# Key and value products cut into two parts, statistics cut from their combination, and new orders for all five engines, in a one-core transformer block

## The chip, the core and the metric

The kernel runs on one core of a Trainium2 chip. Its time is the device time of one execution in microseconds; the median of three runs is the number compared. The core has five engines that run side by side and meet at semaphores: PE (TensorE, matrix products, with its weight loads shown apart as PEld), DVE (VectorE), ACT (ScalarE), POOL (GpSimd) and SP (SyncE, which here only issues DMAs). PE writes to PSUM, eight banks of 512 numbers per partition, from which DVE and ACT read.

## What is computed

The input is a matrix x of 2048 rows (tokens) and 640 columns in bfloat16. A block of linear attention is followed by a dense block, each with a layer norm before it and the input added after it:

```python
h  = x + A(layernorm(x))          # A: linear attention, 32 heads of 20
h2 = h + B(layernorm(h))          # B: silu(h @ w1) @ w2, 1728 wide

def A(x):
    q, k, v = split(x @ wqkv)                     # each 2048 x 640
    pq, pk  = q @ w_phi, k @ w_phi                # per head, 20 x 20
    phi_q   = concat(softmax(pq), softmax(-pq))   # 40 numbers per head
    phi_k   = concat(softmax(pk), softmax(-pk))
    kv, z   = phi_k.T @ v, sum over rows of phi_k # per head 40 x 20 and 40
    return ((phi_q @ kv) / (phi_q @ z)) @ wo
```

## The kernel before

**Tiles.** The tokens are 16 tiles of 128. A tile number is the first number of most steps. The 640 columns are five pieces of 128 where they are contracted over.

**One long list of steps.** The whole program is the string ORDER (L25 to L68): some 620 words, each a call of a small function op_xx, with its arguments behind dots and the PSUM banks it takes behind "@". The words are run from left to right, and each instruction goes to the end of its own engine's queue. Every engine works its queue strictly in that order, so ORDER holds five orders at once, written out in full; only the order of words of the same engine counts. A word whose operand isn't ready holds up all later words of its engine.

**The weights.** wk, wv, wo, w1 and w2 are loaded in pieces (lk, lv, lo, l1, l2; the last rows of w2 by lh) and x in groups of tiles (lx); a last "s" or "a" names the issuing queue, SP or ACT. The small matrices w_phi are folded into the key weights: wt.c transposes piece c of wk on PE (L320), wc.c copies it out of PSUM (L326), ph builds a block-diagonal form of w_phi on DVE (L197) with a mask from mk on POOL, fk.c multiplies the two on PE (L329), and fc.c copies the product to Wfk on ACT (L350). For the queries lq.c loads the weights transposed by DMA, into the same memory as wk (wTq is wk, L135), so lq has to wait until every wt has read wk; gk and gc then do what fk and fc do.

**The layer norm of x.** st.t takes the statistics of the two halves of a tile and combines them, on DVE (L270). rs.a.b makes the reciprocal root of the variance of tiles a to b-1: an add (on DVE for one tile, on POOL for two), then a power and products on POOL (L276 to L291). xn.t normalises, on DVE ("v") or ACT ("a") (L293). Then the tile is transposed: xd.t by a DMA of SP (L313), or xt.t on PE (L304) and xc.t out of PSUM (L310).

**Keys and values.** kp.t and vp.t are the projections of a tile (proj, L366): five pieces times two halves of 320 columns, ten matmuls into a pair of banks. Each of them reads its piece of the transposed tile and of Wfk or wv. ke.t takes the exponentials of both signs on ACT (L392), kr.t their sums per head and the reciprocals on DVE (L401), kn.t the product with them; a letter says how it is shared between POOL and DVE: "p" all on POOL, "q", "b" and "d" three quarters, half and one quarter on POOL, "v" all on DVE (L409). vc.t copies the values out of PSUM. cc.t adds the tile's product of keys and values into bank 7, which collects them over all tiles (L422). kc and km bring the sum into the form used later, with a mask from mt.

**Queries, attention, dense block.** qp, qs, qr and qt are the query projections of four tiles each (L462 to L473), qe their exponentials. dp.t is the product of queries with keys and values, into four banks; dw, dr and do form the quotient (DVE, DVE, DVE or POOL), td transposes it by DMA, op.t multiplies it with wo on PE, and oa.t adds x (DVE). sq, sr, hn and hd are the second layer norm and its transpose. up.g.k are the products with w1 for a group of tiles, ua the silu on ACT, yp and yh the products with w2, yo and yz the last addition and the store.

**Fillers.** wm.n is a product of ones with n columns into an unused bank (L266); eight of 512 columns and six of 256 stand among the first steps.

Of the kernel before, what the change touches and what calls it, by code (L numbers as in the profile page):

```python
# [35 lines left out]
xd.12 vp.12@6 vc.12.v kr.3 kn.3.p kp.4@0 xn.15.a ke.4 kp.12@4 cc.9 cc.1 kr.4 kn.4.p cc.0 xn.14.v cc.11 ke.5
kr.5 kn.2.d xd.13 ke.12 kr.12 lq.4.s xd.6 kp.6@0 lq.0.s ke.6 vp.13@2 vc.13.a kp.13@4 ke.13 vp.6@0 xd.15
xd.10 gk.4@2 vp.10@4 vc.6.a lq.3.s gk.3@0 gc.4.a gc.3.a vc.10.a kn.5.q kp.10@2 kn.12.p kr.6 xn.7.a l1.3.s
kn.6.q lq.1.s gk.1@0 gc.1.a kr.13 kn.13.p cc.4 cc.5 l1.0.s ke.10 kr.10 cc.2 cc.3 cc.12 xd.14 xd.7 kr.8
kn.8.p kn.10.d vp.15@4 vc.15.a kp.15@0 ke.15 kp.14@2 gk.0@4 gc.0.a vp.7@0 ke.14 kr.14 kn.14.p qp.0.1@4  # L40
qs.0.1 qr.0.1 kp.7@2 ke.7 l2.10.13.s kr.15 l1.2.s cc.8 vc.7.v cc.13 l2.2.4.s cc.10 qt.0.1 qp.0.0@2 qs.0.0
kn.15.p qr.0.0 qt.0.0 qe.0.1 l2.4.6.s kr.7 kn.7.v l2.6.8.s qe.0.0 vp.14@0 vc.14.a qp.0.2@6 qs.0.2 cc.6 cc.7
mt qe.0.2 cc.15 cc.14 kc km.0 lh.s qp.3.0@4 qs.3.0 qr.3.0 km.1 dp.0@0 l1.4.s close dw.0.p dr.0 qt.3.0
do.0.1.p qe.3.0 qp.2.0@6 qs.2.0 qr.2.0 qt.2.0 qe.2.0 do.0.0.p dp.1@0 dw.1.p qp.1.0@4 dr.1 do.1.0.p qs.1.0
qr.1.0 qt.1.0 qe.1.0 qp.1.1@6 td.0 do.1.1.p td.1 dp.3@0 dw.3.p dr.3 do.3.0.p qs.1.1 qr.1.1 qt.1.1 qe.1.1
qp.3.2@4 qp.1.2@5 dp.2@0 dw.2.p qs.1.2 qe.1.2 do.3.1.p td.3 qs.3.2 op.0@6 dr.2 do.2.1.p do.2.0.p qe.3.2 oa.0
dp.4@0 dw.4.p td.2 sq.0 qp.2.2@5 qs.2.2 qe.2.2 op.1@6 oa.1 sr.0 qp.2.1@4 dp.6@0 dw.6.p l1.5.s l1.1.s qs.2.1
qr.2.1 hn.0.a hd.0 sq.1 qt.2.1 sr.1 hn.1.v hd.1 qe.2.1 op.3@6 oa.3 sq.3 dp.5@0 dw.5.p op.2@4 sr.3 oa.2
hn.3.a sq.2 dr.5 do.5.0.p do.5.1.p qp.3.1@6 qs.3.1 l2.0.2.s l2.8.10.s qr.3.1 dp.9@0 dw.9.p td.5 dr.9
do.9.0.p dr.6 do.6.1.p dr.4 do.4.1.p do.4.0.p td.4 qt.3.1 qe.3.1 up.0.2@4 ua.0.2 dp.7@0 sr.2 up.0.0@6 ua.0.0  # L50
dw.7.p dr.7 up.0.3@4 ua.0.3 do.6.0.p dp.8@0 dw.8.p dr.8 hn.2.a up.0.1@6 ua.0.1 td.6 do.8.0.p op.5@4 oa.5
dp.12@0 dw.12.p dr.12 yp.1.0@6 do.7.1.p do.7.0.p sq.5 td.7 hd.3 op.4@4 oa.4 sr.5 hn.5.v hd.5 do.9.1.p sq.4
td.9 sr.4 hn.4.a dp.10@0 dw.10.p yp.1.1 yp.0.1@4 yh.0.0 hd.2 hd.4 yo.1 dp.11@0 dw.11.p dr.11 do.8.1.p
do.11.0.p td.8 yp.0.0 yo.0 op.7@6 oa.7 sq.7 dr.10 op.6@0 oa.6 sq.6 sr.6 op.9@2 up.1.6@4 do.11.1.v td.11 oa.9
sq.9 dp.15@0 ua.1.6 sr.9 up.1.5@6 ua.1.5 up.1.1@4 hn.9.v hd.9 do.10.0.p dw.15.p dr.15 hn.6.v hd.6 op.8@6
oa.8 sq.8 op.11@0 ua.1.1 sr.7 hn.7.v hd.7 up.1.3@2 oa.11 do.12.1.p sr.8 hn.8.v do.15.0.p dp.14@4 dw.14.p
dr.14 do.14.0.v hd.8 ua.1.3 up.1.4@0 ua.1.4 do.14.1.v td.14 up.1.0@2 sq.11 sr.11 hn.11.v ua.1.0 up.2.6@4
ua.2.6 dp.13@0 dw.13.p dr.13 do.13.1.p up.2.0@6 up.2.5@4 ua.2.5 op.14@0 up.1.2@2 ua.2.0 oa.14 sq.14 up.2.2@4
ua.1.2 do.12.0.p td.12 sr.14 op.12@6 oa.12 ua.2.2 hn.14.v do.10.1.p do.15.1.v yp.4.0@0 up.2.4@2 ua.2.4 td.10
op.10@4 oa.10 up.2.1@6 sq.12 sr.12 hn.12.a hd.11 hd.12 up.2.3@2 ua.2.1 yp.2.0@4 ua.2.3 yp.9.0@6 do.13.0.p  # L60
td.13 hd.14 yh.2.1@2 td.15 yh.1.0 yp.2.1 yo.2 yp.9.1 yo.9 op.13@4 yp.4.1 yo.4 sq.10 sr.10 yp.6.0@6 op.15@0
hn.10.v hd.10 oa.15 sq.15 sr.15 oa.13 hn.15.a hd.15 yp.7.1 yp.7.0 yo.7 yp.3.0@0 yp.5.0@4 yh.1.1 yh.2.0@2
sq.13 sr.13 yp.6.1 yo.6 yp.3.1 yp.5.1 yo.5 hn.13.v up.4.1@6 hd.13 up.4.2@4 yp.8.1 yp.8.0 ua.4.2 yo.3
up.3.0@0 ua.3.0 yo.8 up.3.3@2 ua.3.3 up.3.5@4 ua.3.5 up.4.0@0 ua.4.0 up.3.1@2 ua.3.1 ua.4.1 up.3.2@4 ua.3.2
up.4.3@0 ua.4.3 yp.14.0@2 yp.15.0@6 up.3.4@4 up.3.6@0 yh.4.0 yp.15.1 ua.3.4 ua.3.6 yp.11.0@4 yp.12.1@0 yo.15
yp.14.1 yo.14 yp.10.1@6 yh.3.1@2,3 yh.3.0 yp.10.0 yo.10 yp.12.0 yo.12 yp.11.1 yo.11 yp.13.0 yz.13.0.s
yp.13.1 yz.13.1.a
"""  # L68

@with_exitstack  # L70
def kernel(
# [194 lines left out]
    def op_wm(n=512):  # L266
        one = nc.const_aps.tensor
        nc.tensor.matmul(mm1()[:, 0:n], one(1.0, (P, P), BF16), one(1.0, (P, n), BF16), start=True, stop=True)  # L268

    def op_st(t):  # L270
        stats = sm.tile([P, 2, 6], F32, name="stats")
        for k in range(2):
            nc.vector.bn_stats(stats[:, k, :], X[:, t, k * 320 : (k + 1) * 320])  # L273
        nc.vector.bn_aggr(MV[:, t, :], stats[:])

    def op_rs(a, b):  # L276
# [86 lines left out]
            tl["gk", ce][:, 1, 0:320].rearrange("p (k r f) -> p k r f", k=2, r=C),  # L363
        )

    def proj(t, W):  # L366
        ps = mm2()
        for c in range(C):
            for half in range(2):
                nc.tensor.matmul(  # L370
                    ps[:, half, 0:320], tok(XnT[t // GT], t)[:, c, :], W[:, c, half * 320 : (half + 1) * 320],
                    start=(c == 0), stop=(c == C - 1),
                )
# [384 lines left out]
```

## Time and profile before

| | |
|---|---|
| median of 3 runs | 236.49 us (236.43 to 236.63) |
| the profiled execution | 236.35 us, of which 234.4 us are the span from the first to the last instruction |
| busy share of PE, DVE, ACT, POOL | 98%, 57%, 49%, 41% |
| DMA | 20.67 MB, a mean of 88 GB/s; 270 GB/s in the first 10 us |

Four views of the profile are used. The page has the span, each engine's busy time, and the chain of work that ended last. The waits list for how long an engine stood, before which line, and what ended it. The timeline has instructions in order of time: start, duration, engine, line, operation, what is written and read, and how many were merged into the row. A row of several instructions spans from the first's start to the last's end. PE's matmuls overlap, so what one takes in a stream is read from the difference of starts and not from its duration. Groups by line give the count, the busy time and the mean in ns, and behind the bar the idle time ahead of them.

### The profile page before, as it was taken

Reading aid. Unit: us, or ns where it says so; the run is one execution under the profiler, and the core shown is the slowest. Engines: PE = TensorE matmul, PEld = TensorE weight load, DVE = VectorE, ACT = ScalarE, POOL = GpSimd, SP = SyncE. Lnnn points to the kernel's source line nnn. Section 1 sums busy time; section 2 is a strip of 40 time slices with the busy share of each in tenths; the row PEclk is TensorE's granted clock in tenths of the full one; section 3 lists DMA queues with packets and bytes.
Section 4 is the critical chain, followed back from the end, with each engine's and each line's share of the span. In section 5 each row is a group of like instructions: output and inputs, shape, how many; then the busy total and the mean of one; then the engine's idle time right before and its main releaser. Section 6 shows DMA issues by size and latency. Waiting matters only on the chain.

```text
span 234.4 us, 6307 instructions
## 1 busy us (share of the span) xinstructions
PE 230.5 (98%) x2674; PEld 148.4 (63%) x2674; DVE 133.5 (57%) x249; ACT 114.5 (49%) x171; POOL 95.4 (41%) x190
## 2 busy tenths in 40 slices
...
GB/s 203 381 234 147 82 112 110 182 64 350 37 3 31 59 176 148 59 49 98 142 55 61 56 3 55 30 57 63 88 24 57 106 27 5 0 3 2 54 34 81
DMA packets 44844, 20.67 MB, mean 88 GB/s; under 512 B 34448, under 2 KB 44304, under 8 KB 44816
## 3 DMA queue, kind: packets, MB, share of 16 engines
...
q14 instruction: 7, 0.06, 0.1%
...
## 4 chain that ended last, share of the span: by engine, by line
PE 98%; ACT 1%; DVE 0%; issue 0%
PE mm L691 24%; PE mm L645 24%; PE mm L370 19%; PE mm L457 10%; PE mm L566 9%; PE mm L504 3%; PE mm L268 2%; PE mm L427 2%; PE mm L337 1%; PE mm L655 1%; PE mm L704 1%; ACT EqT L479 1%; PE mm L322 1%; PE mm L308 0%; DVE ob L721 0%
## 5 line engine op out<-in xcount | busy, mean ns | idle before, releaser
L691 PE MATMUL mm<-w,shT 128*128 128x320 bf16 (+2 forms) x416 | 58.7, 299 | 0.0
L645 PE MATMUL mm<-HnT,w 128*128 128x512 bf16 (+1 forms) x325 | 58.6, 337 | 0.0
L691 PEld LDWEIGHTS <-shT 128*128 128x128 bf16 x416 | 39.6, 98 | 17.2 <-issue 1.1
L667 ACT ACTIVATE shT<-mm 128x1024 bf16<-128x1024 f32 (+2 forms) x29 | 27.6, 963 | 44.6 <-PE mm L645 43.1
L712 DVE TENSOR_TENSOR ob<-mm,X 128x640 bf16<-128x640 f32 x15 | 12.3, 819 | 62.3 <-PE mm L691 59.3
L645 PEld LDWEIGHTS <-w 128*128 128x128 bf16 x325 | 31.4, 98 | 23.2
L370 PEld LDWEIGHTS <-XnT 128*128 128x128 bf16 x320 | 30.8, 98 | 12.0
L414 POOL TENSOR_TENSOR Ek<-Ek,Sk 128x1280 bf16<-128x1280 bf16 (+2 forms) x15 | 32.9, 2217 | 4.0 <-DVE Sk L406 4.0
L539 POOL TENSOR_TENSOR o<-u,rd 128x320 bf16<-128x320 f32 x28 | 19.9, 727 | 22.9 <-DVE rd L533 16.4
L583 ACT ACTIVATE sq<-X 128x640 bf16<-128x640 bf16 x16 | 11.7, 732 | 28.3 <-DVE X L575 27.2
L566 PE MATMUL mm<-wo,ot 128*128 128x320 bf16 x160 | 23.9, 299 | 0.3 <-ACT EqT L479 0.3
L457 PE MATMUL mm<-XnT,Wfq 128*128 128x512 bf16 x100 | 23.8, 380 | 0.0
L370 PE MATMUL mm<-wv,XnT 128*128 128x320 bf16 x160 | 23.7, 299 | 0.0
L370 PE MATMUL mm<-Wfk,XnT 128*128 128x320 bf16 x160 | 23.5, 299 | 0.0
L395 ACT ACTIVATE Ek<-mm 128x640 bf16<-128x640 f32 x32 | 20.5, 714 | 6.0 <-PE mm L370 5.1
L403 DVE TENSOR_REDUCE Sk<-Ek 128x64 f32<-128x1280 bf16 x16 | 23.2, 1452 | 0.3 <-ACT Ek L395 0.3
L479 ACT ACTIVATE EqT<-mm 128x1024 bf16<-128x1024 f32 (+1 forms) x24 | 19.7, 879 | 4.9 <-PE mm L457 4.8
L575 DVE SCALAR_TENSOR_TENSOR X<-mm,X 128x640 bf16<-128x640 f32 x16 | 13.0, 818 | 15.4 <-PE mm L566 15.1
L566 PEld LDWEIGHTS <-ot 128*128 128x128 bf16 x160 | 15.7, 98 | 7.3 <-issue 0.2
L273 DVE BATCH_NORM_STATS2 stats<-X 128x6 f32<-128x320 bf16 x32 | 13.6, 467 | 3.8 <-DMA X<-in_A_x_dram 3.8
L457 PEld LDWEIGHTS <-Wfq 128*128 128x128 bf16 x100 | 9.1, 98 | 9.3
L525 DVE TENSOR_TENSOR u<-mm,w 128x672 f32<-128x672 f32 x16 | 13.7, 857 | 1.2 <-DVE w L523 0.3
...
## 6 DMA issues: line engine op xcount, KB each, us to landing
...
X<-in_A_x_dram SPq DMA_DIRECT2D x3, 640.0 KB, 7.8
...
```

Of the source, the lines that this page charges most:

```text
L370: nc.tensor.matmul(ps[:, half, 0:320], tok(XnT[t // GT], t)[:, c, :], W[:, c, half * 320 : (half + 1) * 320], start=(c == 0), stop=(c == C ...
L395: nc.scalar.activation(Ek[:, s, :].rearrange("p (a n) -> p a n", a=2), tl["kp", t][:, :, 0:320], AF.Exp, scale=1.0 - 2.0 * s,)
L403: nc.vector.tensor_reduce(Sk[:], tl["ek", t][:].rearrange("p s (h f) -> p (s h) f", f=DH), axis=AX.X, op=ALU.add,)
L414: nc.gpsimd.tensor_tensor(Ek3[:, 0:n], Ek3[:, 0:n], Sk[:, 0:n].unsqueeze(2).to_broadcast([P, n, DH]), op=ALU.mult,)
L457: nc.tensor.matmul(tl["qp", g, i][:, k, :], Wfq[:, c, r * P : (r + 1) * P], XnT[g][:, c, :], start=(c == 0), stop=(c == C - 1),)
L479: nc.scalar.activation(E[:, s, rs[0] : rs[-1] + 1, :], tl["qp", g, i][:, 0 : len(rs), :], AF.Exp, scale=1.0 - 2.0 * s,)
L525: nc.vector.tensor_tensor(u[:], A[1][:, :, :, 0:21], w[:].unsqueeze(3).to_broadcast([P, 4, 8, 21]), op=ALU.mult,)
L539: (nc.vector if eng == "v" else nc.gpsimd).tensor_tensor(tl["o", t][:, a * 320 : (a + 1) * 320].rearrange("p (h f) -> p h f", f=DH), tl["u ...
L566: nc.tensor.matmul(ps[:, half, 0:320], tl["ot", t][:, c, :], wo[:, c, half * 320 : (half + 1) * 320], start=(c == 0), stop=(c == C - 1),)
L645: nc.tensor.matmul(ps[:, i * W : (i + 1) * W], w1[:, c, fc * P : (fc + 1) * P], HnT[g][:, c, 0:W], start=(c == 0), stop=(c == C - 1), skip ...
L667: nc.scalar.activation(sh[:, a:b], tl["up", g, k][:, 0 : b - a], AF.Silu)
L691: nc.tensor.matmul(ps, shT[g][:, fc * W + i * P : fc * W + (i + 1) * P], w2[:, fc, a:b], start=first and fc == 0, stop=last and fc == FC - ...
```

## The change

No mathematics changes, and no weight or tile is cut otherwise.

- proj takes the PSUM pair and a range of pieces. kp.t and vp.t now issue the first three pieces (six matmuls), and the new words kq.t and vq.t the last two (four matmuls), so that other words of PE can stand between.
- st.t is cut: the new word sa.t takes the statistics of the first half, st.t those of the second half and the combination.
- ORDER is another list throughout, for all engines. Two fillers (256 and 128 columns) are added behind wt.1. ph stands behind the statistics of tile 1 instead of before them. xn.0 and wc.4 go from DVE to ACT. wt.4 and xt.0 stand ahead of all fk, and fk.4 behind the first part of kp.0. lq.2 stands ahead of the loads of tiles 4 to 7 and 12 to 15, lh behind these. Of the xn, 2, 8, 9 and 12 go from ACT to DVE, and 0 and 5 from DVE to ACT; vc.7 and vc.12 go to ACT. The kn are shared otherwise: before kn.2 and kn.10 were "d", kn.5 and kn.6 "q", kn.7 "v"; after kn.7 and kn.13 are "d" and kn.5 and kn.14 "b"; the others are "p". In the dense half, the op and up words stand in another order, dp keeps banks 2 to 5 for long stretches instead of 0 to 3, and some hn and do change their engine.

```diff
 ORDER = """
-mk mo lx.0.1.a lk.0.1.s lp.a lx.1.2.s lk.4.5.a wm.512@7 wm.512@7 wm.512@7 wm.512@7 wm.512@7 wm.512@7
-wm.512@7 wm.512@7 wt.0@0 lk.1.2.s ta wc.0.a wm.256@2 wm.256@2 wm.256@2 wm.256@2 wm.256@2 wm.256@2 wt.1@1 wc.1.a st.0 rs.0.1
-ph.v fk.0@2 fc.0.a st.1 lk.2.3.s wt.2@4 wc.2.v lk.3.4.s wt.3@5 wc.3.v fk.1@6 fc.1.a rs.1.2 fk.2@0 fc.2.a
-lx.2.4.s xn.0.v lx.8.12.s wt.4@4 wc.4.v lv.0.3.s fk.3@2 fc.3.a xt.0@5 xn.1.v xc.0.v st.2 fk.4@6 fc.4.a
-rs.2.3 lv.3.5.s mc.0 xt.1@4 xc.1.a st.9 st.8 rs.8.10 lx.4.8.s st.3 rs.3.4 kp.0@0 ke.0 xn.2.a kp.1@2 ke.1
-lx.12.16.s vp.1@6 st.10 xt.2@5 vp.0@0 xc.2.a xn.9.a vc.0.a vp.2@2 st.11 lo.2.5.s xn.3.v xt.3@4 xc.3.a
...
+lx.0.1.a sa.0 st.0 mo lk.0.1.s lp.a wm.512@7 wm.512@7 wm.512@7 wm.512@7 wm.512@7 wm.512@7 wm.512@7 wm.512@7
+wt.0@0 mk rs.0.1 lx.1.2.s lk.4.5.a lk.1.2.s lk.2.3.s lk.3.4.s wm.256@2 wm.256@2 wm.256@2 wm.256@2 wm.256@2
+wm.256@2 wt.1@1 wm.256@3 wm.128@3 wt.2@2 lx.2.4.s ta wc.0.a xn.0.a sa.1 st.1 rs.1.2 wc.1.a lx.8.12.s wt.4@3
+xt.0@4 wc.4.a ph.v fk.0@6 fc.0.a fk.1@0 fc.1.a wt.3@5 wc.2.v fk.2@2 xn.1.v xt.1@6 lv.0.3.s xc.0.v wc.3.v
+fk.3@4 sa.2 fc.2.a kp.0@0 xc.1.a st.2 rs.2.3 sa.3 st.3 rs.3.4 fc.3.a fk.4@2 fc.4.a lv.3.5.s kp.1@6 lq.2.s
+kq.1 lx.4.8.s lx.12.16.s xn.2.v sa.8 kq.0 ke.0 lh.s xt.2@4 xc.2.a mc.0 sa.9 st.9 st.8 sa.10 xn.3.v vp.1@2
+vq.1 vc.1.a vp.0@0 vq.0 vc.0.a sa.11 st.11 rs.8.10 xn.9.v xt.3@5 vp.2@2 st.10 rs.10.12 xd.9 xn.8.v kp.2@0
+sa.5 st.5 kq.2 sa.4 st.4 lq.4.s xc.3.a ke.1 ke.2 vq.2 vc.2.a xd.8 kp.3@4 xn.11.v xd.11 gk.2@6 gc.2.a sa.13
+mc.1 lq.1.s rs.4.6 kq.3 ke.3 xn.5.a sa.12 st.12 st.13 vp.3@0 vq.3 xd.5 kr.1 vp.9@2 vq.9 l1.2.s xn.4.a xd.4
...
+kn.15.p cc.6 vp.7@4 vq.7 vc.7.a mt qp.0.2@6 cc.15 cc.14 kr.7 kn.7.d cc.7 qs.0.2 kc qp.3.0@0 qs.3.0 qr.3.0
...
+dw.11.p dr.11 hd.2 sr.4 hn.4.a hd.4 yp.0.0 yo.0 op.7@0 oa.7 sq.7 op.8@2 oa.8 sq.8 dr.12 op.9@4 oa.9 dr.10
+dp.15@0 op.6@6 oa.6 dw.15.p dr.15 do.11.0.p do.10.1.p sr.8 do.11.1.v up.1.4@4 sq.6 up.1.3@6 ua.1.3 sr.6
...
 """
...
+    def op_sa(t):
+        tl["stats", t] = sm.tile([P, 2, 6], F32, name="stats")
+        nc.vector.bn_stats(tl["stats", t][:, 0, :], X[:, t, 0:320])
+
     def op_st(t):
-        stats = sm.tile([P, 2, 6], F32, name="stats")
-        for k in range(2):
-            nc.vector.bn_stats(stats[:, k, :], X[:, t, k * 320 : (k + 1) * 320])
+        stats = tl["stats", t]
+        nc.vector.bn_stats(stats[:, 1, :], X[:, t, 320:D])
         nc.vector.bn_aggr(MV[:, t, :], stats[:])
...
-    def proj(t, W):
-        ps = mm2()
-        for c in range(C):
+    def proj(t, W, ps, cs):
+        for c in cs:
             for half in range(2):
                 nc.tensor.matmul(
                     ps[:, half, 0:320], tok(XnT[t // GT], t)[:, c, :], W[:, c, half * 320 : (half + 1) * 320],
                     start=(c == 0), stop=(c == C - 1),
                 )
-        return ps
 
     def op_vp(t):
-        tl["vp", t] = proj(t, wv)
+        tl["vp", t] = mm2()
+        proj(t, wv, tl["vp", t], range(3))
+
+    def op_vq(t):
+        proj(t, wv, tl["vp", t], range(3, C))
...
     def op_kp(t):
-        tl["kp", t] = proj(t, Wfk)
+        tl["kp", t] = mm2()
+        proj(t, Wfk, tl["kp", t], range(3))
+
+    def op_kq(t):
+        proj(t, Wfk, tl["kp", t], range(3, C))
```

68 lines of the change are left out of this document (32 added, 36 removed).

## The prediction

> **What bounds the kernel now.** I read the head of the page, the chain that ended last, the waits of TensorE alone, and then the first 15 us engine by engine in order of time.
>
> ```profile
> span 234.4 us, 6307 instructions
> PE 230.5 (98%) x2674; PEld 148.4 (63%) x2674; DVE 133.5 (57%) x249; ACT 114.5 (49%) x171; POOL 95.4 (41%) x190
> PE 98%; ACT 1%; DVE 0%; issue 0%
> PE mm L566 <- ACT EqT L479: 0.3, 1, 0.3
> ```
>
> The first three lines are from the page, the last from the waits of PE: 0.3 us, once, near 88 us, is all that it waited once it had begun. Whatever the other engines do counts only where it makes PE wait. The timeline of PE shows where more time hides, as small holes that no wait row names:
>
> ```profile
> 4.73 1.49 PE L268 MATMUL mm<-const-bfloat16-1.0 128*128 128x256 bf16 x6
> 6.25 0.45 PE L322 MATMUL mm<-ident,wk 128*128 128x128 bf16 x5
> 8.21 0.44 PE L322 MATMUL mm<-ident,wk 128*128 128x128 bf16 x5
> 8.49 0.48 PE L337 MATMUL mm<-phb,wTk 128*128 128x140 bf16 x6
> 8.80 0.44 PE L308 MATMUL mm<-ident,xn 128*128 128x128 bf16 x5
> 9.99 2.89 PE L370 MATMUL mm<-Wfk,XnT 128*128 128x320 bf16 x20
> 12.72 1.52 PE L370 MATMUL mm<-wv,XnT 128*128 128x320 bf16 x10
> ```
>
> From 9.99 us (kp.0) to its last matmul PE streams. The diff leaves every matmul of that stretch in number, shape and operands: kp and vp are cut in two but issue the same ten matmuls. So a gain can come from the start alone, and the question is when PE has done what it had done at 12.72 us (all wt and fk, xt.0, xt.1, kp.0, kp.1), and whether it stalls afterwards.
>
> **The start, PE alone.** Differences of starts give a transpose group 0.28 us (8.21 to 8.49), an fk 0.31 (8.49 to 8.80), a full kp 1.365 (9.99 to 12.72 for two), so 0.82 for its first three pieces and 0.55 for the other two. wt.1 started at 6.25, on the landing of the second piece of wk; the loads up to there keep their order, so it stays. From then on the work is 4 x 0.28 + 5 x 0.31 + 2 x 0.28 + 2.73 = 5.96 us, which without any wait ends at 12.21. Before needed until 12.72, so 0.5 us were holes. The two new fillers, 256 and 128 columns, take by the six of 256 between 4.73 and 6.25 at most 0.37 us, and sit in front of wt.2, where PE may wait anyway. The best that the start can give is therefore about -0.4 us.
>
> **The start, ScalarE.** This is where I expect the gain to go.
>
> ```profile
> 3.83 0.89 DVE L273 BATCH_NORM_STATS2 stats<-X 128x6 f32<-128x320 bf16 x2 [3.83 <-DMA X<-in_A_x_dram]
> 5.00 0.15 DVE L278 TENSOR_SCALAR RS<-MV 128x1 f32<-128x1 f32 x1
> 5.08 0.99 DVE L198 TENSOR_TENSOR phb<-phr,mask 128x800 bf16<-128x800 bf16 x1
> 5.24 1.24 POOL L281 TENSOR_TENSOR RS<-RS,nhalf 128x1 f32<-128x1 f32 x1 [0.75 <-DVE RS L278]
> 6.58 0.26 POOL L283 TENSOR_SCALAR RS<-MV,RS 128x1 f32<-128x1 f32 x1
> 11.24 0.55 POOL L281 TENSOR_TENSOR RS<-RS,nhalf 128x1 f32<-128x1 f32 x1 [1.66 <-DVE RS L278]
> 11.89 0.26 POOL L283 TENSOR_SCALAR RS<-MV,RS 128x1 f32<-128x1 f32 x1
> 6.74 0.69 ACT L171 COPY wTk<-mm 128x640 bf16<-128x640 bf16 x1 [1.07 <-PE mm L322]
> 7.33 3.17 ACT L171 CAST Wfk<-mm 128x640 bf16<-128x640 f32 x5
> 10.35 0.74 ACT L171 COPY XnT<-mm 128x640 bf16<-128x640 bf16 x1
> 27.31 1.76 ACT L302 ACTIVATE xn<-X,RS 128x640 bf16<-128x640 bf16 x2
> 12.74 0.92 ACT L302 ACTIVATE xn<-X,RS 128x640 bf16<-128x640 bf16 x1
> 64.63 0.70 ACT L171 CAST Vp<-mm 128x640 bf16<-128x640 f32 x1
> ```
>
> After the change ACT runs wc.0, xn.0, wc.1, wc.4, fc.0, fc.1, fc.2, xc.1, fc.3, fc.4 in that order; xn.0 and wc.4 are taken over from DVE. xn.0 waits for the rstd of tile 0. The add on DVE ends at 5.15 in both kernels. The power on POOL took 1.24 us beside phb, but 0.55 at 11.24. Now ph comes behind the statistics of tile 1 on DVE, so I take the pair of 11.24 (0.91 us from its start to the end of L283): rstd is there at 5.24 + 0.91 = 6.15, and xn.0 starts at 6.2. In a row, ACT's steps are 0.84 for xn (two in 1.76, one 0.92), 0.59 for a wc (6.74 to 7.33), 0.62 for an fc (five in 3.17, a single cast 0.70) and as much for xc.1. So fc.4 ends at 6.2 + 0.84 + 2 x 0.59 + 3 x 0.62 + 0.62 + 0.62 + 0.70 = 12.02. PE meanwhile gets phb 1.25 us later, at 7.3 (3.83 to 5.08 is what one tile's statistics, their combination and the add take), and DVE brings wc.2, xn.1, xc.0 and wc.3 behind it, four steps of 0.5 us at most, so that fk.3 and then kp.0 come by about 9.7. It then runs fk.4, kp.1 and the first two matmuls of kq.1, and waits for fc.4: it has the last two of kq.1 and the four of kq.0 left, 6 x 0.136 = 0.82 us, with 0.06 to get going. It is through at 12.90 instead of 12.72: **+0.2 us**. The split does start kp.0 some 0.3 us sooner; the longer row of work on ACT takes it back.
>
> Bounds: with each of ACT's ten steps at its own duration (0.92, 0.69, 0.70, 0.74) the row is 6.54 us long, not 5.82, which adds 0.7; with the power still at 1.24 xn.0 starts at 6.9, which adds 0.7; with no wait at all it is -0.4. I keep +0.2, since the short durations are what this engine shows back to back.
>
> Two readings of the 1.24 us are open. POOL's first power, of four elements at 1.44 us with DVE idle, took 1.03, so the second may have been slow for being early, and then ph's new place gains nothing:
>
> ```profile
> 1.44 1.03 POOL L147 TENSOR_TENSOR ones<-ones,nhalf 128x4 f32<-128x4 f32 x1
> ```
>
> The Trainium skill, "SBUF — State Buffer", section "Who interferes with whom", says that a VectorE instruction with two SBUF inputs and a GpSimd instruction that reads SBUF exclude each other for the whole instruction. By that rule the power waited for phb's end at 6.07 and ran 0.41 us, in keeping with the row of 0.55; the start would come out as summed, and the same lock would now hold tile 1's power instead. By the reading of a slow early power the sum is +0.9.
>
> **After the start.** Each later handoff keeps its engine row but a new distance, so I compared PE's work between producer and user with the duration in between, and looked at the shortest.
>
> ```profile
> 13.55 1.30 ACT L395 ACTIVATE Ek<-mm 128x640 bf16<-128x640 f32 x2
> 38.20 1.32 PE mm L427 x128
> 83.83 0.82 DVE L575 SCALAR_TENSOR_TENSOR X<-mm,X 128x640 bf16<-128x640 f32 x1
> ```
>
> vp.0 takes the banks of kp.0 with 1.64 us between (xt.2 and 1.36), ke.0 needs 1.30. kp.2 takes vp.0's banks 1.10 us after vq.0, vc.0 needs 0.70. cc.7 follows vq.7 by 1.10 us (qp.0.2 and two cc of 0.33), vc.7 needs 0.70. dp.15 takes the bank pair of op.8 1.36 us after it, oa.8 needs 0.82, but stands on DVE behind yo.0 and oa.7, and I make it just in time. All hold, by 0.1 to 0.4 us. The stall near 88 us (op.2 behind qe.2.1) has the same order of PE and ACT around it and stays. From dp.0 to dp.7 the PE order is the same but for one swap.
>
> DVE is nearly PE's equal in the last part of the key stage, and must not lose there (the first row gives the busy time of PE, PEld, DVE, ACT and POOL from 50 to 65 us):
>
> ```profile
> 50.00:65.00 15.00, 15.00 (x208) 9.45 (x195) 14.50 (x15) 10.32 (x16) 12.01 (x6) 1.00 0.59 173
> L418 DVE TENSOR_TENSOR Ek<-Ek,Sk 128x960 bf16<-128x960 bf16 x2 | 2.4, 1212 | 0.0
> L418 DVE TENSOR_TENSOR Ek<-Ek,Sk 128x320 bf16<-128x320 bf16 x2 | 1.3, 648 | 0.1
> L418 DVE TENSOR_TENSOR Ek<-Ek,Sk 128x1280 bf16<-128x1280 bf16 x1 | 1.9, 1924 | 0.0
> L169 DVE CAST Vp<-mm 128x640 bf16<-128x640 f32 x2 | 1.6, 795 | 0.6 <-PE mm L370 0.6
> L297 DVE TENSOR_SCALAR xn<-X,MV,RS 128x640 bf16<-128x640 bf16 x5 | 2.3, 468 | 0.0
> L414 POOL TENSOR_TENSOR Ek<-Ek,Sk 128x1280 bf16<-128x1280 bf16 x11 | 26.9, 2456 | 4.0 <-DVE Sk L406 4.0
> ```
>
> It gives up kn parts (2 x 1.21 + 2 x 0.65 + 1.92), two vc (1.6), wc.4 (0.5) and two xn (0.9), 8.6 us; it gets kn parts (2 x 1.21, and two halves that I put between the rows at 0.93) and four xn (1.9), 6.2 us. So the last kn on DVE, tile 7's, gains some 2.4 us on its cc, of which mt, now in front of it, takes a part back. POOL takes over the half kn that DVE gives up in all, some 1.2 us at 2.46 for a whole one, in a stretch where it was 12.0 of 15 us busy. Cutting statistics from their combination adds no instruction: it is free.
>
> SP is the other place. lq.2 now stands in front of the loads of tiles 4 to 7 and 12 to 15, and it waits until the last wt has read wk:
>
> ```profile
> 21.71 1.23 SPq L251 DMA_TRANSPOSE wk<-in_A_wqkv_dram  x1
> wk<-in_A_wqkv_dram SPq DMA_TRANSPOSE x5, 3.1
> X<-in_A_x_dram SPq DMA_DIRECT2D x1, 640.0 KB, 7.8
> 5.98 1.11 SPq L236 DMA_DIRECT2D X<-in_A_x_dram  x2
> ```
>
> The load of tiles 4 to 7 was issued at 5.98 and landed 7.8 us later, at 13.8. Now wt.3 is done near 8.5, lq.2 issues for 1.23, the load goes out near 9.8 and lands between 15 and 17.6 (the same 7.8). DVE wants it at sa.5, behind the statistics of six tiles (0.9 to 1.1 us each) and four xn (0.47) that begin near 9.5, so at 17 to 18. No wait in the likely case, and one of 1 us would come off the 2.4 us that DVE gained.
>
> **Sum.** +0.2 from the start, 0 to +0.2 from handoffs, nothing else. On the profiled execution (236.35 us, span 234.4) that is 236.55 to 236.75; the median of the runs shown is 236.49, 0.14 above it. I predict **236.7 us**.
>
> **Rivals.**
> - *ScalarE bounds the start outright.* The steps of ACT at their own durations, or the slow power: +0.9 each, +1.6 both; 237.4. It decides where fc.4 ends after 12.3, which is where +0.2% begins. For it: 1.03 and 1.24 for the first two powers. Against: 0.55 for a later one. 0.25.
> - *The loads behind lq.2 come late.* sa.5 then holds DVE, and with it the statistics of tiles 12 and 13, whose rstd ACT wants for xn.13 ahead of ke.9 and so of vp.11; I count some 1.5 us of room on that path. If the 7.8 us grow by the whole 3.1 of lq.2, tiles 4 to 7 land at 20.7, over 3 us after sa.5 is due: +1.5, 238.0 (median). It decides from a landing after 19. For it: the loads share their queue with the transpose. Against: they go out 3.8 us later, when less stands ahead of them. 0.10.
> - *The start runs without holes.* -0.4, and with the 0.3 of the stall at 88 us also gone 235.8. For it: kp.0 no longer needs fc.3 and fc.4. Against: it needs ACT to be quicker than any row here. 0.13.
> - *The change does nothing that counts*: kp.0 sooner, all else given back exactly: 236.5; part of the forecast.
>
> **Numbers.** 0.2% of 236.49 is 0.47 us, about what a measurement of this kernel can tell from no change. Forecast 0.52 (236.3 to 236.95, all within). Slower: 0.25 + 0.10 of the first two rivals. The third has 0.13, of which 0.10 is faster by over 0.2% and 0.03 within. So faster 0.10, same 0.55, slower 0.35. The range, 236.1 to 237.5, holds the forecast and the first rival at its single price; it leaves out the doubled ones and most of the other two.
>
> **What would show it.** Right: xn.0 on ACT at 6.2 with a power of 0.6 us before it; fc.4 ending near 12.0; kq.0 done by 12.9; PE unbroken to the end but for 88 us. Wrong: fc.4 after 12.5, a wait of PE on ACT or DVE between 13 and 66 us, sa.5 waiting for a DMA, or the second half of a kp standing with its operands ready.

## The result, and the profile after

The changed kernel takes **236.92 us** (median of 15 runs, 236.83 to 237.56), the kernel before on the same chip 236.43 (15 runs, 236.13 to 236.73). The ratio is 1.0023, with a 95% interval from 1.0015 to 1.0030: slower by 0.23%, just past the 0.2% that bounded "within". The profiled execution has a span of 235.0 us against 234.4.

Line numbers have moved by 2 to 11: L270 is the filler, L327 wt, L342 fk, L313 xt, L374 the projections, L425 and L429 kn on POOL and on DVE, L230 the two copies of mt, L438 cc, L468 the query products, L577 op.

First the page's head and chain, then the waits of PE:

```profile
span 235.0 us, 6302 instructions
PE 230.1 (98%) x2676; PEld 148.1 (63%) x2676; DVE 131.3 (56%) x250; ACT 114.2 (49%) x172; POOL 96.1 (41%) x188
...
PE 70%; ACT 1%; DVE 0%; POOL 0%; issue 0%
```

```profile
PE mm L438 <- POOL Ek L425: 0.6, 1, 0.6
...
PE mm L577 <- ACT EqT L490: 0.3, 1, 0.3
```

The last row is the old stall near 88 us, unchanged. The first is new: for 0.6 us PE stands before a cc (L438) and is released by POOL's part of a kn (L425). The two rows left out lie in the first 6 us: 0.8 us before the first filler, and 0.4 before wt.1, for a landing. The chain is followed back to that part of the kn, at 65.3 us, and no further: PE's 70% is the stretch behind it.

**The start.** PE, then ACT, in order of time:

```profile
9.56 1.03 PE L374 MATMUL mm<-Wfk,XnT 128*128 128x320 bf16 x6
...
10.75 2.16 PE L374 MATMUL mm<-Wfk,XnT 128*128 128x320 bf16 x14
12.74 0.44 PE L313 MATMUL mm<-ident,xn 128*128 128x128 bf16 x5
```

```profile
6.23 0.92 ACT L307 ACTIVATE xn<-X,RS 128x640 bf16<-128x640 bf16 x1 [0.60 <-POOL RS L288]
7.06 1.26 ACT L173 COPY wTk<-mm 128x640 bf16<-128x640 bf16 x2
8.21 1.89 ACT L173 CAST Wfk<-mm 128x640 bf16<-128x640 f32 x3
9.96 0.73 ACT L173 COPY XnT<-mm 128x640 bf16<-128x640 bf16 x1
10.55 1.33 ACT L173 CAST Wfk<-mm 128x640 bf16<-128x640 f32 x2
```

What PE had done at 12.72 before (kp.0 and kp.1 with all that they need) it has done at 12.74 now, when xt.2 begins: **+0.02**. ACT's row has no gap from xn.0 at 6.23 to the end of fc.4 at 10.55 + 1.33 = 11.88. POOL's powers and the DVE product beside them:

```profile
5.29 0.54 POOL L286 TENSOR_TENSOR RS<-RS,nhalf 128x1 f32<-128x1 f32 x1 [0.94 <-DVE RS L283]
...
6.52 1.24 POOL L286 TENSOR_TENSOR RS<-RS,nhalf 128x1 f32<-128x1 f32 x1 [0.32 <-DVE RS L283]
```

```profile
6.36 0.99 DVE L200 TENSOR_TENSOR phb<-phr,mask 128x800 bf16<-128x800 bf16 x1
```

The 1.24 us has moved with ph, from tile 0's power to tile 1's, where nobody waits for it. Both times the power ends 0.41 us behind phb (6.48 and 6.07 before, 7.76 and 7.35 now).

**The stall.** PE, DVE and POOL of the kernel after around 65 us, and the same place on POOL and DVE of the kernel before:

```profile
64.71 0.66 PE L438 MATMUL mm<-Ek,Vp 128*21 128x40 bf16 x64
65.95 0.37 PE L438 MATMUL mm<-Ek,Vp 128*21 128x40 bf16 x32 [0.58 <-POOL Ek L425]
```

```profile
63.74 1.27 DVE L429 TENSOR_TENSOR Ek<-Ek,Sk 128x960 bf16<-128x960 bf16 x1
```

```profile
57.36 6.63 POOL L425 TENSOR_TENSOR Ek<-Ek,Sk 128x1280 bf16<-128x1280 bf16 x3 [0.69 <-ACT Ek L406]
63.94 1.32 POOL L230 COPY KVBD<-maskS 128x15 bf16<-128x15 bf16 x2
65.18 0.72 POOL L425 TENSOR_TENSOR Ek<-Ek,Sk 128x320 bf16<-128x320 bf16 x1
```

```profile
65.91 0.40 POOL L228 COPY KVBD<-maskS 128x15 bf16<-128x15 bf16 x2 [2.00 <-DVE maskS L224]
```

```profile
63.33 1.92 DVE L418 TENSOR_TENSOR Ek<-Ek,Sk 128x1280 bf16<-128x1280 bf16 x1
65.18 0.67 DVE L224 STREAM_TRANSPOSE maskS<-maskR 128x480 bf16<-128x480 bf16 x1
```

cc.7 could begin at 64.71 + 0.66 = 65.37. DVE's three quarters of kn.7 are there at 65.01. POOL's quarter is not: it stands behind kn.15 (to 63.99) and mt's two copies, which take 1.32 us here and 0.40 before, and it ends at 65.90. PE goes on at 65.95, **+0.58**. Before, kn.7 was wholly on DVE and the copies came behind it, when POOL had been idle for 2.00 us. The sum, 0.02 + 0.58 = 0.60, agrees with the difference of the spans (235.0 and 234.4).

### The profile page after: what moved, and what is told of

Same layout as the page of the kernel before. It is cut to its first block, busy times and chain, and to the rows that moved or that the text cites. A ratio compares the mean times of both kernels' runs of the same rounds, so it can differ in the third digit from the quotient of the medians.

```text
span 235.0 us, 6302 instructions
## 1 busy us (share of the span) xinstructions
PE 230.1 (98%) x2676; PEld 148.1 (63%) x2676; DVE 131.3 (56%) x250; ACT 114.2 (49%) x172; POOL 96.1 (41%) x188
## 4 chain that ended last, share of the span: by engine, by line
PE 70%; ACT 1%; DVE 0%; POOL 0%; issue 0%
PE mm L702 24%; PE mm L656 24%; PE mm L577 9%; PE mm L468 8%; PE mm L515 3%; PE mm L666 1%; PE mm L715 1%; ACT EqT L490 1%; DVE ob L732 0%; POOL Ek L425 0%; PE mm L438 0%
## 5 line engine op out<-in xcount | busy, mean ns | idle before, releaser
L374 PEld LDWEIGHTS <-XnT 128*128 128x128 bf16 x320 | 30.6, 98 | 12.0
L550 POOL TENSOR_TENSOR o<-u,rd 128x320 bf16<-128x320 f32 x25 | 18.7, 764 | 41.8 <-DVE rd L544 35.4
L425 POOL TENSOR_TENSOR Ek<-Ek,Sk 128x1280 bf16<-128x1280 bf16 (+2 forms) x16 | 33.6, 2118 | 4.5 <-DVE Sk L417 2.9
L374 PE MATMUL mm<-Wfk,XnT 128*128 128x320 bf16 x160 | 24.5, 299 | 0.0
L577 PE MATMUL mm<-wo,ot 128*128 128x320 bf16 x160 | 23.7, 300 | 0.3 <-ACT EqT L490 0.3
L468 PE MATMUL mm<-XnT,Wfq 128*128 128x512 bf16 x100 | 24.0, 380 | 0.0
L374 PE MATMUL mm<-wv,XnT 128*128 128x320 bf16 x160 | 23.5, 299 | 0.0
L577 PEld LDWEIGHTS <-ot 128*128 128x128 bf16 x160 | 15.3, 98 | 6.9 <-issue 0.2
L468 PEld LDWEIGHTS <-Wfq 128*128 128x128 bf16 x100 | 9.1, 98 | 9.2
L539 DVE TENSOR_TENSOR u<-u,mm 128x672 f32<-128x672 f32 x16 | 13.6, 853 | 0.6
```

The source lines that it names most:

```text
L374: nc.tensor.matmul(ps[:, half, 0:320], tok(XnT[t // GT], t)[:, c, :], W[:, c, half * 320 : (half + 1) * 320], start=(c == 0), stop=(c == C ...
L425: nc.gpsimd.tensor_tensor(Ek3[:, 0:n], Ek3[:, 0:n], Sk[:, 0:n].unsqueeze(2).to_broadcast([P, n, DH]), op=ALU.mult,)
L468: nc.tensor.matmul(tl["qp", g, i][:, k, :], Wfq[:, c, r * P : (r + 1) * P], XnT[g][:, c, :], start=(c == 0), stop=(c == C - 1),)
L550: (nc.vector if eng == "v" else nc.gpsimd).tensor_tensor(tl["o", t][:, a * 320 : (a + 1) * 320].rearrange("p (h f) -> p h f", f=DH), tl["u ...
L577: nc.tensor.matmul(ps[:, half, 0:320], tl["ot", t][:, c, :], wo[:, c, half * 320 : (half + 1) * 320], start=(c == 0), stop=(c == C - 1),)
```

## The experiments

Three theories went into them. **P**: the stall is made where it shows, by mt's copies and POOL's part of kn.7 standing beside DVE's part. **U**: DVE and POOL come to tile 7 late from further up, where ke.14 starts late and DVE waits for it. **S**: the loss sits in the start. To see where a difference arises I also read TensorE's place: the start of op.3 in each profile (the L577 row near 86 us), which lies behind everything that the runs touch. It is that of one execution. "xt.2" is the end of the start.

| kernel | median, us | before beside it | ratio (95%) | xt.2 | op.3 |
|---|---|---|---|---|---|
| before | | | | (12.72) | 86.10 |
| after | 236.92 | 236.43 | 1.0023 (1.0015 to 1.0030) | 12.74 | 86.73 |
| e1_mt_late | 236.45 | 236.37 | 1.0001 (0.9993 to 1.0010) | 12.78 | 86.48 |
| e2_kn7_dve | 236.23 | 236.37 | 0.9996 (0.9987 to 1.0005) | 12.67 | 86.08 |
| e4_ph_early | 237.54 | 236.37 | 1.0042 (1.0028 to 1.0056) | 13.52 | 87.53 |
| e5_before_mt_early | 236.76 | 236.37 | 1.0017 (1.0008 to 1.0025) | (12.43) | 86.26 |
| e9_cc_early | 237.19 | 236.28 | 1.0039 (1.0027 to 1.0052) | 12.87 | 86.94 |
| e6_unsplit_start | 237.03 | 236.28 | 1.0029 (1.0018 to 1.0040) | 13.47 | 86.92 |
| e7_unsplit_rest | 237.25 | 236.28 | 1.0044 (1.0028 to 1.0060) | 12.66 | 87.11 |
| e10_start | 236.63 | 236.28 | 1.0017 (1.0008 to 1.0025) | 12.80 | 86.24 |
| e11_keys_whole | 237.65 | 236.26 | 1.0056 (1.0043 to 1.0069) | 12.80 | 87.63 |
| e12_values_whole | 236.22 | 236.26 | 1.0001 (0.9992 to 1.0010) | 12.69 | 86.12 |
| e13_stats_whole | 236.13 | 236.26 | 0.9993 (0.9985 to 1.0002) | 12.87 | 86.27 |

In brackets: vp.1's start, which in the order of before is the same point. The medians follow the places with 149.9 to 150.5 us between them, so a difference of 0.3 us between two medians can still be that of two executions.

### mt behind kn.7 (e1_mt_late)

```diff
-... vc.7.a mt qp.0.2@6 cc.15 cc.14 kr.7 kn.7.d cc.7 ...
+... vc.7.a qp.0.2@6 cc.15 cc.14 kr.7 kn.7.d mt cc.7 ...
```

> The order of after, with one step moved: mt (a transpose on DVE and two small copies on POOL) from in front of kr.7 to behind kn.7. Theory P (POOL's quarter of tile 7's kn stands on POOL behind mt's two copies, which run beside DVE's quarter-less kn and take 1.32 us instead of 0.40; that makes the whole stall of 0.58 us at cc.7): the copies leave POOL's row ahead of kn.7, POOL starts its part as soon as DVE's kr.7 is done (63.7), the stall at 65.95 goes, and the time falls by 0.5 to 0.6 us, to 236.3 to 236.5, even with the kernel before. Theory U (DVE's and POOL's rows are late from further up, by the wait of ke.14 for a free Ek buffer at 51.2; mt only sits in the place where it shows): DVE's kr.7 and kn.7 still end after 65.4 or POOL is still busy with kn.15, and at least 0.3 of the 0.58 us stays. Theory S (the loss sits in the start, where the rows of ScalarE are longer): nothing changes beyond 0.1 us.

Half of it. DVE, POOL and PE:

```profile
63.25 1.83 DVE L429 TENSOR_TENSOR Ek<-Ek,Sk 128x960 bf16<-128x960 bf16 x1
```

```profile
61.71 2.36 POOL L425 TENSOR_TENSOR Ek<-Ek,Sk 128x1280 bf16<-128x1280 bf16 x1
64.02 1.64 POOL L425 TENSOR_TENSOR Ek<-Ek,Sk 128x320 bf16<-128x320 bf16 x1
65.73 0.40 POOL L230 COPY KVBD<-maskS 128x15 bf16<-128x15 bf16 x2
```

```profile
65.72 0.37 PE L438 MATMUL mm<-Ek,Vp 128*21 128x40 bf16 x32 [0.28 <-POOL Ek L425]
```

The copies are out of the way and take 0.40 again, but POOL's quarter (the second row) still ends only at 65.66, 0.58 behind the end of DVE's part at 65.08. The stall is 0.28 instead of 0.58. The copies make 0.30 of it, where theory P had given them all; the rest is the shared kn itself. DVE gained nothing by the step taken from it: its product began 0.49 us sooner than in after (63.25 against 63.74) and ended 0.07 later, as kn.15 ran on POOL until 64.07.

### kn.7 whole on DVE (e2_kn7_dve)

```diff
-... vc.7.a mt qp.0.2@6 cc.15 cc.14 kr.7 kn.7.d cc.7 ...
+... vc.7.a mt qp.0.2@6 cc.15 cc.14 kr.7 kn.7.v cc.7 ...
```

> The order of after, with tile 7's kn whole on DVE (as before had it), mt still in front of it. Theory P: POOL has no part in cc.7 any more; DVE's kn.7 takes 1.9 us from 63.7 and ends near 65.65, beside mt's copies on POOL perhaps a little later; cc.7, which could start at 65.37, waits 0.2 to 0.35 us on DVE instead of 0.58 on POOL; time 0.25 to 0.4 below after. Theory U: the same place waits for DVE, for about as long as now (0.5 us or more), and the time stays within 0.1 of after. Theory S: no change of time either way; the stall would shift but not the end.

Better than either theory said: no stall that the waits list names.

```profile
63.66 1.60 DVE L429 TENSOR_TENSOR Ek<-Ek,Sk 128x1280 bf16<-128x1280 bf16 x1
```

```profile
63.87 1.66 POOL L230 COPY KVBD<-maskS 128x15 bf16<-128x15 bf16 x2
```

```profile
64.64 1.05 PE L438 MATMUL mm<-Ek,Vp 128*21 128x40 bf16 x96
```

```profile
65.32 0.38 PE L438 MATMUL mm<-Ek,Vp 128*21 128x40 bf16 x32
```

The three cc run as one row; cc.7, the last of them, is shown by itself as well. All 1280 columns take DVE 1.60 us, less than 960 in e1 beside POOL (1.83), and end at 65.26. PE still waits a little: cc.7 starts 0.06 us behind that end, and the row takes 1.05 us where three cc take 0.92 in e5's row and 0.93 in e11's (both below), so some 0.13 us is left that no wait row names. U falls as the whole cause: with POOL out of tile 7's kn, DVE is all but in time with everything further up as it was. S falls too: the start is that of after (12.67 and 12.74), and the loss is gone. The time, 236.23, is level with before. This is the order of after with one letter changed.

### The converse in the kernel before (e5_before_mt_early)

```diff
-kn.15.p qr.0.0 qt.0.0 qe.0.1 l2.4.6.s kr.7 kn.7.v ... cc.6 cc.7 mt qe.0.2 ...
+kn.15.p qr.0.0 qt.0.0 qe.0.1 l2.4.6.s mt kr.7 kn.7.d ... cc.6 cc.7 qe.0.2 ...
```

> The order of before, with the end of its key stage as after has it: mt in front of kr.7, and tile 7's kn three quarters on DVE and a quarter on POOL. Nothing of the start is touched. Theory P: POOL meets mt's two copies beside DVE's part, its quarter comes late, a wait of PE on POOL of 0.2 to 0.6 us appears near 65.5 us in a stretch that had none, and the time goes up by that, to 236.7 to 237.0. Theory U: before has no wait of ke.14 for a buffer as late as after's, so DVE and POOL come to this place sooner and the same steps cost at most 0.1 us. Theory S: no change.

```profile
65.57 0.92 PE L427 MATMUL mm<-Ek,Vp 128*21 128x40 bf16 x96 [0.21 <-POOL Ek L414]
```

```profile
63.57 0.40 POOL L228 COPY KVBD<-maskS 128x15 bf16<-128x15 bf16 x2
63.88 1.64 POOL L414 TENSOR_TENSOR Ek<-Ek,Sk 128x320 bf16<-128x320 bf16 x1
```

```profile
63.74 1.19 DVE L418 TENSOR_TENSOR Ek<-Ek,Sk 128x960 bf16<-128x960 bf16 x1
```

As P said, at the low end: a stall on POOL of 0.21 where before had none, and 236.76 against 236.37. The copies came just ahead of DVE's part and ran in 0.40; this time POOL's quarter met it, took 1.64 and ended at 65.52, 0.59 behind the end of DVE's (64.93).

So one reading covers all four kernels. POOL's instruction beside DVE's product ends a fixed time behind it, whatever its own start: the copies by 0.25 (after: 63.94 + 1.32 against 65.01) and 0.27 us (e2: 65.53 against 65.26), the quarter by 0.58 and 0.59. Tile 13's kn, shared in the same way, shows it once more in after: POOL's quarter took 1.64 and ended at 61.68, DVE's part at 61.09. By these rows POOL's instruction waits for the end of DVE's and then runs. It holds the other way round too. DVE's product of tile 7 began before kn.15 had ended on POOL in before, after, e1 and e2, and it ended a fixed time behind kn.15 whatever its own start: 960 columns 1.02 (after: 65.01 and 63.99) and 1.01 us (e1: 65.08 and 64.07), 1280 columns 1.35 us twice (before: 65.25 and 63.90; e2: 65.26 and 63.91). "SBUF — State Buffer" of the Trainium skill, section "Who interferes with whom", says of a VectorE instruction with two SBUF inputs and a GpSimd instruction that reads SBUF that they contend, and that the one that issues first holds the other up for its whole length; these rows agree. kn.15 on POOL, in before and in e2:

```profile
61.55 2.35 POOL L414 TENSOR_TENSOR Ek<-Ek,Sk 128x1280 bf16<-128x1280 bf16 x1
```

```profile
61.56 2.35 POOL L425 TENSOR_TENSOR Ek<-Ek,Sk 128x1280 bf16<-128x1280 bf16 x1
```

### ph back beside the first power (e4_ph_early)

```diff
-... ta wc.0.a xn.0.a sa.1 st.1 rs.1.2 ... wc.4.a ph.v fk.0@6 ...
+... ta wc.0.a xn.0.a ph.v sa.1 st.1 rs.1.2 ... wc.4.a fk.0@6 ...
```

> The order of after, with ph (the product of phase and mask on DVE, 0.99 us, two inputs in SBUF) put back directly behind the combination of tile 0's statistics, where before had it, so that it runs beside POOL's first power for a tile. If the power takes 1.24 us because a DVE operation with two SBUF inputs stands beside it: the power of tile 0 shows about 1.2 us again and that of tile 1 about 0.55, xn.0 starts at 6.9 instead of 6.23 us, and ScalarE's row behind it ends 0.5 to 0.7 us later, fc.4 at 12.4 to 12.6; TensorE gets through the start 0.4 to 0.7 us later than 12.74, and the time rises by as much unless the stall at cc.7 takes it up (that stall waits on POOL behind DVE's tile 15 work, which hangs on TensorE's products, so it should not). If the first power is slow for another reason (early, cold): 0.54 us in this place too, and phb 1 us sooner at no loss: the time is the same or up to 0.2 lower.

```profile
5.36 1.24 POOL L286 TENSOR_TENSOR RS<-RS,nhalf 128x1 f32<-128x1 f32 x1 [0.99 <-DVE RS L283]
...
7.51 0.54 POOL L286 TENSOR_TENSOR RS<-RS,nhalf 128x1 f32<-128x1 f32 x1 [0.55 <-DVE RS L283]
```

```profile
7.00 0.92 ACT L307 ACTIVATE xn<-X,RS 128x640 bf16<-128x640 bf16 x1 [1.33 <-POOL RS L288]
```

The two durations have changed places, xn.0 starts 0.77 later, xt.2 0.78 later, and the time is 237.54 (0.62 above after). The prediction's first reading of the 1.24 us is shown: the power waited for phb, and was not slow for being early. It ends 0.40 us behind phb here (6.60 and 6.20). The stall at cc.7 stays at 0.58, so it does not take up a loss further up.

### Two cc earlier (e9_cc_early)

```diff
-... gk.3@4 gc.3.a kn.5.b kq.14 kp.6@0 lo.0.2.s l2.8.10.s cc.5 kr.13 l1.3.s kn.4.p kn.10.p cc.3 cc.4 ke.14 ...
+... gk.3@4 gc.3.a cc.3 kn.5.b kq.14 cc.5 kp.6@0 lo.0.2.s l2.8.10.s kr.13 l1.3.s kn.4.p kn.10.p cc.4 ke.14 ...
```

> The order of after, with two of the sums of keys and values, cc.3 and cc.5, about one projection further up on TensorE (cc.5 in front of the first part of kp.6, cc.3 in front of kq.14). Nothing of tile 7's kn or of mt is touched. In after the exponentials of tile 14 start at 51.7 us, half way through a block of five cc, and DVE stands 1.45 us for them before it goes on with kr.14, kr.6, kr.15 and kr.7. Theory U (the stall at cc.7 comes from there: DVE and POOL arrive late at tile 7): ke.14 starts near 50.5, DVE's wait shrinks to 0.4 or less, POOL is done with kn.15 and mt's copies before cc.7 is due, the stall of 0.58 us goes or shrinks below 0.2, time 236.3 to 236.5. Theory P alone (what costs is mt's copies and POOL's part standing beside DVE's part, wherever in time): DVE and POOL may come sooner, but tile 7's own products then bound kr.7, and the stall stays at 0.4 or more; time within 0.15 of after. If ke.14 waits for something else than a cc, its start stays at 51.7.

```profile
66.18 0.37 PE L438 MATMUL mm<-Ek,Vp 128*21 128x40 bf16 x32 [0.41 <-POOL Ek L425]
```

```profile
51.08 1.30 ACT L406 ACTIVATE Ek<-mm 128x640 bf16<-128x640 f32 x2 [0.42 <-PE mm L374]
```

ke.14 did start 0.7 us sooner (51.08 against 51.78). But DVE then waited at kr.14 for 0.62 us, put down to POOL, and at kr.6 for 0.78 us, and began tile 7's kn only 0.18 sooner against PE's cc (1.15 us ahead of the group instead of 0.97): the stall is 0.41. U explains 0.17 of the 0.58, no more. The time is worse, 237.19. PE's place is lost by 0.13 in the start and by the two more changes between projections and cc: the groups of 50 to 52 us start 0.09 to 0.11 us later than a plain stream would have them, each time a cc follows a projection.

### The cut of kp.0 undone (e6_unsplit_start; base here and below: e2)

```diff
-fk.3@4 sa.2 fc.2.a kp.0@0 xc.1.a ... fc.3.a fk.4@2 fc.4.a lv.3.5.s kp.1@6 lq.2.s kq.1 ... sa.8 kq.0 ke.0 ...
+fk.3@4 sa.2 fc.2.a xc.1.a ... fc.3.a fk.4@2 fc.4.a kp.0@0 kq.0 lv.3.5.s kp.1@6 lq.2.s kq.1 ... sa.8 ke.0 ...
```

> The order of after with tile 7's kn whole on DVE (which showed no stall at cc.7), and the cut of kp.0 undone: fk.4 stands ahead of kp.0, and kq.0 right behind kp.0. If the cut earns at the start what ScalarE's longer row costs: kq.0 has to wait for the last copy of the folded weights, fc.4 at 11.8, with kp.1 and kq.1 (ten matmuls, 1.37 us) behind it, so xt.2 starts at 13.4 to 13.6 instead of 12.67, and the time is 0.7 to 0.9 above that kernel's 236.23, at 236.9 to 237.1. If the cut is worth nothing: xt.2 within 0.2 us of 12.67 and the time within 0.2.

```profile
11.84 1.79 PE L374 MATMUL mm<-Wfk,XnT 128*128 128x320 bf16 x12 [0.16 <-ACT Wfk L173]
```

kq.0 waits for fc.4, and the twelve matmuls from its last two on stand behind that wait. +0.80 at xt.2 and +0.80 in the median (237.03 against 236.23): in this order the cut earns 0.8 us, which ACT's longer row and the later fk.4 would otherwise cost.

### The start eased on ACT (e10_start)

```diff
-xt.0@4 wc.4.a ph.v ... wc.2.v fk.2@2 ... wc.3.v fk.3@4 sa.2 fc.2.a kp.0@0 xc.1.a ... fc.3.a fk.4@2 fc.4.a
+xt.0@4 ph.v ... wc.2.v wc.4.v fk.2@2 ... wc.3.v sa.2 fc.2.a kp.0@0 fk.3@4 xc.1.a ... fk.4@2 fc.3.a fc.4.a
```

> The order of after with tile 7's kn whole on DVE, and the start eased on ScalarE: wc.4 back on DVE (between wc.2 and xn.1), and kp.0 in front of fk.3, with fk.4 right behind fk.3. If ScalarE's row up to fc.1 holds back kp.0, as the forecast had it: fc.1 ends near 9.05 instead of 9.4, kp.0 starts near 9.1, fc.4 ends near 11.6, and xt.2 starts at 12.4 to 12.5 instead of 12.67: time 0.2 below that kernel, about 236.0, if DVE's later half microsecond does not come back as a wait at cc.7 (it has 1.4 us idle before kr.14). If TensorE alone bounds the start: xt.2 within 0.05 of 12.67 and no change.

A miss. PE and ACT:

```profile
9.27 1.03 PE L374 MATMUL mm<-Wfk,XnT 128*128 128x320 bf16 x6 [0.16 <-DVE wTk L171]
```

```profile
10.65 1.29 ACT L173 CAST Wfk<-mm 128x640 bf16<-128x640 f32 x2 [0.24 <-PE mm L342]
```

kp.0 came 0.2 sooner, but ACT now waits for PE: 0.28 us ahead of fc.0, since wc.4 no longer fills the time until fk.0 is done, and 0.24 ahead of fc.3, since fk.3 stands behind kp.0. So fc.4 ends at 11.94 instead of 11.81. Five kernels with the cut of kp.0 agree on this start: xt.2 begins 0.86 us behind the end of fc.4 (11.81 and 12.67 in e2, 11.88 and 12.74 in after, 11.92 and 12.78 in e1, 11.94 and 12.80 in e10, 12.66 and 13.52 in e4).

### The other cuts undone (e7_unsplit_rest, e11_keys_whole, e12_values_whole, e13_stats_whole)

In e7 every kq and vq (but kq.0 and kq.1) stands right behind its kp or vp and every sa in front of its st; e11, e12 and e13 do one of the three each. One line of e11, where kq.8, kq.5 and kq.12 move:

```diff
-kp.11@2 ... sa.14 kp.8@4 kp.5@0 ke.11 gk.4@6 gc.4.a kq.8 xn.10.a ke.8 ... kq.5 ke.5 ... kp.12@4 ... vq.12 kq.12
+kp.11@2 ... sa.14 kp.8@4 kq.8 kp.5@0 kq.5 ke.11 gk.4@6 gc.4.a xn.10.a ke.8 ... ke.5 ... kp.12@4 kq.12 ... vq.12
```

> The order of after with tile 7's kn whole on DVE, and every other cut undone: each kq and vq right behind its kp or vp (but for tiles 0 and 1 of the keys), each sa right in front of its st. TensorE's work between 13 and 60 us is the same matmuls in a slightly other order, and it streams there. Forecast: no difference by over 0.15 us from that kernel's 236.23, and no new wait of TensorE over 0.1 us. If the cuts hide waits in the key stage: waits on ACT or DVE at kp, vp or cc between 13 and 60 us, 0.2 us or more in sum.

> The order of after with tile 7's kn whole on DVE, and only the cuts of the key products undone from tile 2 on: each kq right behind its kp. Undoing all cuts but the start's had cost 1.0 us by TensorE's position at 86 us (87.11 against 86.08), against the forecast of none. If the cuts of the keys carry it (kq.14 and kq.6, which give the copies and exponentials of the pairs ahead time to end, and move kp.6's second part behind the five cc): a gap of 0.2 to 0.3 us ahead of kp.14, cc.5 half a microsecond later, waits of about 0.2 each on POOL and DVE near 62 and 66 us; xt.2 unchanged at 12.67 and the position at 86 us near 86.9 to 87.1; time 0.7 to 1.0 above 236.23. If values or statistics carry it: position within 0.2 of 86.08.

> The order of after with tile 7's kn whole on DVE, and only the cuts of the value products undone: vq.2 and vq.4 right behind vp.2 and vp.4 (the others stand there already). If keys carry the loss of 1.0 us: the position at 86 us stays within 0.2 of 86.08 and the time within 0.25 of 236.23. If values carry a part: a gap ahead of kp.12 or vp.12 near 34 us, of about 0.15 us.

> The order of after with tile 7's kn whole on DVE, and only the cut of the statistics undone: each sa right in front of its st, no other word moved. No instruction is added or taken away on DVE, and its order changes by half a tile's statistics (0.43 us) at ten places. Forecast: nothing, position at 86 us within 0.1 of 86.08, time within 0.2 of 236.23. If the first halves fill waits of DVE for loads or powers: DVE's key work comes later by some tenths, and a wait at the kn or cc appears, 0.2 us or more.

The forecast for e7 was wrong: 237.25, 1.0 us above e2 in the median and in PE's place. Values and statistics are nothing, as forecast (86.12 and 86.27, the latter with xt.2 0.20 later); the keys carry it all. PE and ACT in e11, then ACT in e2:

```profile
34.50 1.52 PE L374 MATMUL mm<-Wfk,XnT 128*128 128x320 bf16 x10 [0.52 <-ACT Ek L406]
...
63.20 0.93 PE L438 MATMUL mm<-Ek,Vp 128*21 128x40 bf16 x96 [0.21 <-POOL Ek L425]
...
66.87 0.30 PE L438 MATMUL mm<-Ek,Vp 128*21 128x40 bf16 x21 [0.26 <-DVE Ek L429]
```

```profile
31.69 0.75 ACT L173 CAST Wfq<-mm 128x320 bf16<-128x320 f32 x2 [0.98 <-PE mm L342]
```

```profile
30.48 0.76 ACT L173 CAST Wfq<-mm 128x320 bf16<-128x320 f32 x2
```

With kq.8 and kq.5 whole ahead of gk.4, ACT gets gc.4 1.21 us later, and with it xn.10 and ke.8; kp.12 wants ke.8's banks and waits. So a cut of the contraction is a place to put in a short product that feeds another engine (gk.4 here) before the long one is done. This accounts for 0.52 of e11's loss of 1.42 in the median; two more waits, 0.21 at cc.13 and 0.26 at cc.7, lie behind it, and how they come from the keys is not traced. e7 undoes more than e11 and is faster (87.11 against 87.63): there vq.4 stands whole in front of kp.12, which has no wait row, and the difference of the two places is 0.52 us as well.

## Why the prediction was right and wrong

The number came close (236.7 forecast, 236.92 measured, inside the range), but with another cause: the start cost 0.16 us less than forecast, and a stall that stood in no term of the sum cost 0.58. That the number is no further off is in part luck. Of the forecast's own split at 0.2%, the result falls just inside "slower" (0.35) and not in the likelier "same" (0.55), though its interval, 0.15% to 0.30%, has the line within it. Its sign "PE unbroken to the end but for 88 us" failed.

**Right.** The bound: PE streams to the end and only what makes it wait counts. The power at 0.54 behind the moved ph, xn.0 at 6.23 (forecast 6.2), the row of ACT without a gap and its end at 11.88 (12.02), PE's rest of 0.86 behind it (0.88). That the cut of kp.0 takes up ACT's longer row: 0.8 us without it (e6). The loads behind lq.2: issued at 9.8 as forecast, and sa.5 begins at 17.18 without a wait, so that rival is out. The handoffs that it lists hold: no wait row names one of them. The 88 us stall stays.

**Mis-sized: the start**, +0.18 forecast and +0.02 measured against that profile. ACT's row from xn.0 to the end of fc.4 took 5.65 us (6.23 to 11.88) instead of 5.82, which is nearly all of the difference. And the reference itself moves. In before, wt.1 started on the landing of the second piece of wk, as the prediction read it, but that this "stays" does not hold. The weight loads of wt.1, in before and then in e5, which has the same words up to there:

```profile
6.25 0.28 PEld L322 LDWEIGHTS <-wk 128*128 128x128 bf16 x5 [0.51 <-DMA wk<-in_A_wqkv_dram]
```

```profile
5.95 0.28 PEld L322 LDWEIGHTS <-wk 128*128 128x128 bf16 x5 [0.24 <-DMA wk<-in_A_wqkv_dram]
```

In e5 the piece landed sooner, and wt.1 (5.96 against 6.25) and vp.1 (12.43 against 12.72) come 0.29 sooner with it. So the new start is level with the old one in one execution and 0.3 behind it in another; this part of the comparison stays open by that much.

**Wrong: the step on DVE and POOL at the end of the key stage**, "the last kn on DVE, tile 7's, gains some 2.4 us on its cc, of which mt, now in front of it, takes a part back", with POOL's additional 1.2 us placed "in a stretch where it was 12.0 of 15 us busy", and nothing for it in the sum. Four things were wrong in it.

- The 2.4 us was busy time given up, not time gained. From 50 to 65 us DVE went from 14.50 to 13.27 busy, but kn.7's end came from 65.25 to 65.01 only. The time given up became idle time further up, 1.45 us of it ahead of kr.14. Nor would an earlier DVE have helped: its product of tile 7 ended a fixed time behind kn.15 on POOL, which ended at 63.90 before and 63.99 after. The window's row (PE, PEld, DVE, ACT, POOL), and the wait on DVE:

```profile
50.00:65.00 15.00, 15.00 (x405) 9.78 (x403) 13.27 (x14) 10.78 (x16) 13.57 (x8) 1.00 0.08 24
```

```profile
53.18 1.49 DVE L414 TENSOR_REDUCE Sk<-Ek 128x64 f32<-128x1280 bf16 x1 [1.45 <-ACT Ek L406]
```

- POOL's load was taken as a mean over 15 us (12.0, now 13.57). What counts is its queue at one place: kn.15 until 63.99, then the copies, then the quarter for which cc.7 waits.
- mt was counted on DVE alone. Its two copies are POOL's, and they now stand ahead of a kn.
- The list of handoffs has cc.7 with its values alone (vc.7, 1.10 us against 0.70). Its other operand, kn.7, for which it then waited, is not in the list.

That one engine waits for the other's instruction, by which I priced the power at 6 us, I did not apply to the same two engines at 64 us, where POOL's copies and quarter meet DVE's product. By the rows shown it makes the whole stall of 0.58: 0.30 through the copies (e1), 0.28 through the quarter itself, and neither is left with kn.7 on one engine (e2).

The rival in which ScalarE bounds the start has its mechanism shown (the 0.86 us behind fc.4, and e4), but not its condition: fc.4 ended at 11.88, ahead of 12.3. No rival of mine was the one that came.
